# Windowed decode attention and a gated block on one core: one exponential per group with mask products, w4's last rows split over DMA engines, one load for the last rows of wo

## The chip, the core and the metric

The kernel runs on one core of a Trainium2 chip. Its time is device microseconds; the median of three runs of the kernel before is 193.25 us (193.23 to 193.55).

## What is computed

One decode step. A row x of 512 is normalised; s is sliding window attention of 32 heads over the last 4,096 of 32,768 cached positions, with 128 features per head; g is a small gated block of matrix products on the same row; the output is x + s * silu(g). All inputs are bf16.

```python
q = (x @ wq).reshape(...)                     # 32 heads of 128, from xn
k, v = k_cache[:, :, Sk - W:, :], v_cache[:, :, Sk - W:, :]     # W = 4096
scores = einsum("bhqd,bhkd->bhqk", q, k) * Dh ** -0.5
p = softmax(scores, axis=-1)
s = einsum("bhqk,bhkd->bhqd", p, v).reshape(...) @ wo
# the block: h = gelu(layernorm(xn) @ w1), shifted by a position or two;
# with one position nothing of it is left, so hs = 0
x1 = xn + hs
h2 = gelu(layernorm(x1) @ w3) @ w4
out = x + s * silu(x1 + h2)
```

## The kernel before

**Tiling.** The 32 heads go in eight groups of G = 4. A group's K is one tile of 128 partitions by 128 positions by 128 features (4 MB); partition 4b + a holds the positions of head a in block b, so that a partition belongs to one head of the four. V is laid out in the same way. Three K tiles and two V tiles are held at a time.

**Stages of a group.** Step s of the main loop works on the scores of group s, the softmax of group s - 1 and the values of group s - 2 (LAG = 2).

- k_vector (L316 to L323) computes the scores of the first 64 or 80 positions of each partition on VectorE, in four parts: a product with q (L321) and a sum (L323) into S.
- k_turn (L339, L342) and k_scores (L350) compute those of the other 48 or 64: TensorE transposes K, ScalarE copies the result, and TensorE multiplies it with q of all four heads into sT. Each row of sT then has four scores of which one, that of the partition's head, counts. Groups 0 and 7 have 64 positions here and the others 48.
- sm_own (L354 to L359) multiplies sT with the mask par (1 where the head is the partition's) on ScalarE, four instructions. sm_max (L364, L366) adds the four up into S and takes the row's maximum m1.
- sm_turn (L368 to L376) turns m1 onto one partition (TensorE), takes a maximum for each head (mx), and writes minus the scaled maximum into the first row of md, whose four other rows hold 0 on the diagonal and -1e30 off it.
- sm_exp (L378 to L389): a TensorE product of par_t and md gives every partition four offsets, the right one for its own head and about -1e30 for the other heads. ScalarE then makes four exponentials of S, one for each offset, so that those of other heads come out as 0, with their sums.
- sm_den, sm_rden (L394, L399): sums over partitions, reciprocal.
- v_wide (L423 to L433) multiplies pT with V into ov and copies it to SBUF, v_turn (L444) transposes it, v_add (L450) adds up, v_out (L464 to L475) multiplies with the reciprocal into o. For groups 3 to 7 v_out is one instruction on VectorE, for 0 to 2 four on ScalarE.
- ox_spread, ox_pick and y_wide (L478 to L520) bring o into the layout of the product with wo, for heads 0 to 15 (in step 6), 16 to 23 (steps 7 and 8) and 24 to 27 (steps 8 and 9). Heads 28 to 31 go by y_head (L522) with the rows wo_rows. warm (L504) runs matmuls whose result is not used.

**Order.** Order on TensorE, VectorE and ScalarE is that of the program (a manual schedule, L527 to L649), and each engine waits in that order. All large loads but wq are issued by SyncE in the order of the program (L75, L76): w2, w3, w4, then K 0, 1, 2, V 0, K 3, V 1 and so on, each when its buffer is free; wq comes from ScalarE's queue. V 7 is loaded in three pieces, cuts = (0, 64, 96, 128), behind which stand two loads of wo_rows (L542, L543). In step 9 the last piece of V 7 is multiplied by v_part (L458), then v_out(7), four y_head, the product with silu (L651), the sum (L653) and the store.

The order of step 8, and the places where ox_spread follows v_out:

```python
            if h > 0:
                v_add(h - 1)
                v_out(h - 1)
            if s == 6:
                ox_spread(0)
            k_vector(s, kn, 3)
...
        elif s == NG:
            ox_pick(1)
            sm_turn(NG - 1)
            sm_exp(NG - 1)
            y_wide(1, False)
            sm_den(NG - 2)
            sm_rden(NG - 2)
            y_wide(0, False)
            warm(3)
            v_wide(h, v)
```

In step 7, v_add(5), v_out(5), ox_spread(1) and sm_max(7) are the last of VectorE.

Of the kernel before, what the change touches and what calls it, by code (L numbers as in the profile page):

```python
# [8 lines left out]
P = 128  # L9
BF16 = mybir.dt.bfloat16  # L10
FP32 = mybir.dt.float32
ACT = mybir.ActivationFunctionType
# [6 lines left out]
G = 4  # L19
LAG = 2  # L20
K_BUFS = 3
V_BUFS = 2
LATE = 7


@with_exitstack
def kernel(
# [42 lines left out]
    sm_pool = ctx.enter_context(tc.tile_pool(name="sm", bufs=3))  # L70
    small.tile([P, 96], BF16, name="pad")
    wts_guard = tc.tile_pool(name="wts", bufs=1)
    wts = wts_guard.__enter__()

    def load(dst, src):  # L75
        return tc.keep_in_program_order(nc.sync.dma_start(out=dst, in_=src))  # L76
# [14 lines left out]
    load(w4_sb[:, 0:10, :], B_w4[0:10 * P, :].rearrange("(p c) n -> p c n", p=P))  # L91
    load(w4_sb[0:96, 10, :], B_w4[10 * P:F, :])

# [27 lines left out]
    neg_half = const.tile([P, 33], FP32, name="neg_half")  # L121
    nc.vector.memset(neg_half[:], -0.5)

# [104 lines left out]
    shifted_bf = small.tile([P, KC], BF16, name="shifted_bf")  # L228
    nc.vector.memset(shifted_bf[:], 0.0)
    hs_ps = ps_misc.tile([P, KC], FP32, tag="misc", name="hs_ps")  # L230
# [16 lines left out]
    for c in range(KC):  # L247
        wc = w3_sb[:, c, 0:10 * P].rearrange("p (q r) -> p r q", r=10)
        parts = [(j, a_ps[32 * j:32 * j + 1, :, :], wc[:, 3 * j:3 * j + 3, :]) for j in range(3)]
        parts += [(3, a_ps[96:97, 0, :], wc[:, 9, :]), (3, a_ps[96:97, 1, 0:96], w3_sb[:, c, 10 * P:F])]  # L250
        for j, dst, w in parts:
            nc.tensor.matmul(dst, lhsT=z3_bf[:, c:c + 1], rhs=w, start=False, stop=(c == KC - 1),
                             skip_group_check=True)
# [14 lines left out]
    for i, (col, w) in enumerate(terms):  # L268
# [28 lines left out]
                            op=ALU.max)  # L297
    par_t = const.tile([1 + G, PB, G], FP32, name="par_t")
    nc.vector.tensor_scalar(out=par_t[:],
                            in0=ident_f[0:1 + G, 1:1 + G].unsqueeze(1).to_broadcast([1 + G, PB, G]),  # L300
                            scalar1=ident_f[0:1 + G, 0:1], scalar2=None, op0=ALU.add)
    md = const.tile([1 + G, G], FP32, name="md")
    nc.vector.tensor_scalar(out=md[:], in0=ident_f[0:1 + G, 1:1 + G], scalar1=-1.0, scalar2=1e30,
                            op0=ALU.add, op1=ALU.mult)

    st = {}

    def nd(g):
        return 64 if g == 0 or g >= LATE else 80

    def k_open(g):
        st[g] = {
            "sT": ps_s.tile([P, CP - 64, G], FP32, tag="sT", name="sT"),
            "S": sm_pool.tile([P, CP], FP32, tag="S", name="S"),
        }
# [37 lines left out]

    def sm_own(g):  # L354
        s = st[g]
        m = CP - nd(g)
        s["own"] = sm_pool.tile([P, CP - 64, G], FP32, tag="own", bufs=1, name="own")
        for a in range(G):
            nc.scalar.mul(s["own"][:, 0:m, a], s["sT"][:, 0:m, a], par[:, a:a + 1])  # L359

    def sm_max(g):
        s = st[g]
        n = nd(g)
        nc.vector.tensor_reduce(out=s["S"][:, n:CP], in_=s["own"][:, 0:CP - n, :], axis=AX.X, op=ALU.add)  # L364
        s["m1"] = sm_pool.tile([P, 1], FP32, tag="m1", name="m1")
        nc.vector.tensor_reduce(out=s["m1"][:], in_=s["S"][:], axis=AX.X, op=ALU.max)  # L366

    def sm_turn(g):  # L368

        s = st[g]  # L370
        mt_ps = ps_misc.tile([1, P], FP32, tag="misc", name="mt_ps")
        nc.tensor.transpose(mt_ps[:], s["m1"][:], ident_f[:])  # L372
        mx = sm_pool.tile([1, G], FP32, tag="mx", name="mx")
        nc.vector.tensor_reduce(out=mx[:], in_=mt_ps[:].rearrange("r (b a) -> r a b", a=G), axis=AX.X,  # L374
                                op=ALU.max)
        nc.vector.tensor_scalar(out=md[0:1, :], in0=mx[:], scalar1=-scale, scalar2=None, op0=ALU.mult)  # L376

    def sm_exp(g):  # L378
        s = st[g]
        mb_ps = ps_misc.tile([P, G], FP32, tag="misc", name="mb_ps")  # L380
        nc.tensor.matmul(mb_ps[:], lhsT=par_t[:].rearrange("k b a -> k (b a)"), rhs=md[:], start=True,  # L381
                         stop=True)
        mb = sm_pool.tile([P, G], FP32, tag="mb", name="mb")
        nc.scalar.copy(out=mb[:], in_=mb_ps[:])  # L384
        s["pT"] = sm_pool.tile([P, CP, G], BF16, tag="pT", name="pT")
        s["sum"] = sm_pool.tile([P, G], FP32, tag="sum", name="sum")
        for a in range(G):
            nc.scalar.activation(out=s["pT"][:, :, a], in_=s["S"][:], func=ACT.Exp, scale=scale,  # L388
                                 bias=mb[:, a:a + 1], accum_out=s["sum"][:, a:a + 1])  # L389

    def sm_den(g):
        s = st[g]
        s["den"] = ps_misc.tile([P, G], FP32, tag="misc", name="den_ps")
        nc.tensor.matmul(s["den"][:], lhsT=ones_f[:], rhs=s["sum"][:], start=True, stop=True)  # L394

    def sm_rden(g):
        s = st[g]
        s["rden"] = sm_pool.tile([P, G], FP32, tag="rden", name="rden")
        nc.vector.reciprocal(out=s["rden"][:], in_=s["den"][:])  # L399
# [14 lines left out]
    def load_rows(h, n):  # L414
        load(wo_rows[:, h - h_part:h - h_part + n, :],
             A_wo[h * P:(h + n) * P, :].rearrange("(h p) n -> p h n", p=P))
# [29 lines left out]
    def v_add(g):  # L446
        s = st[g]
        if g < NG - 1:
            s["oT"] = sm_pool.tile([P, G], FP32, tag="oT", name="oT")
        nc.vector.tensor_reduce(out=s["oT"][:], in_=s["ot"][:].rearrange("p (x m) -> p m x", m=32)[:, 0:G, :],  # L450
                                axis=AX.X, op=ALU.add)
# [12 lines left out]
    def v_out(g):  # L464
        h = G * g
        b = [i for i, (h0, _) in enumerate(blocks) if h >= h0][-1]
        if b not in o_blk:
            o_blk[b] = sm_pool.tile([P, blocks[b][1]], BF16, tag=f"o{b}", bufs=1, name="o")
        c = h - blocks[b][0]
        if g >= NG - 5:  # L470
            nc.vector.tensor_tensor(out=o_blk[b][:, c:c + G], in0=st[g]["oT"][:], in1=st[g]["rden"][:],
                                    op=ALU.mult)
            return
        for k in range(G):
            nc.scalar.mul(o_blk[b][:, c + k:c + k + 1], st[g]["oT"][:, k:k + 1], st[g]["rden"][:, k:k + 1])  # L475

# [54 lines left out]
    for s in range(NG + LAG):  # L531
# [8 lines left out]
        if last:  # L540
            v = load_kv(v_pool, A_v_cache, h, cuts)
            for r in (H - G, H - 2):  # L542
                load_rows(r, 2)  # L543
        elif h >= 0:
            v = load_kv(v_pool, A_v_cache, h)
# [8 lines left out]
        if s < NG:  # L554
# [32 lines left out]
            k_scores(s, nb - 1)  # L587
            sm_own(s)
            if s == 7:
# [95 lines left out]
```

## Time and profile before

| what | value |
|---|---|
| median of three runs | 193.25 us |
| span of the profiled execution (the page gives this time of it) | 191.2 us |
| TensorE matmul, weight load busy | 116.4, 74.2 us (61, 39%) |
| VectorE busy | 150.9 us (79%) |
| ScalarE busy | 89.2 us (47%) |
| GpSimd busy | 2.3 us (1%) |
| moved by DMA | 79.02 MB, mean 413 GB/s |
| chain that ended last | VectorE 46%, DMA 43%, TensorE 5%, ScalarE 3% |

The page divides the span into 40 slices and gives the busy share of each engine in tenths. The chain of work that ended last is followed back from the last instruction, at each step to what released it. A group of instructions has its line, engine, operation, output and inputs, shape and count, then busy time, mean duration in ns, and the idle time of the engine ahead of it with its cause. A row in order of time has start and length in us. TensorE matmuls are pipelined and their ends are modelled.

### The profile page before, as it was taken

The page shows a single profiled execution, that of the slowest core. Times are in us where ns is not written, and L with a number is a line of the kernel's source. Part 1 is how long each engine was busy: PE and PEld are TensorE (multiplying, and loading weights), DVE is VectorE, ACT ScalarE, POOL GpSimd, SP SyncE. Part 2 cuts the span into 40 slices and gives each one's busy share as a digit, 9 for nine tenths or more (in the row PEclk, how much of TensorE's full clock was granted, in tenths as well). Part 3 has the DMA queues.
Part 4 walks back from the last instruction along what each step waited for, and adds up shares of the span by engine and source line. Part 5 has one row for each costly group of instructions (what it writes and reads, how often), then busy time and mean ns, then how long its engine had stood idle before and what let it go on. Part 6 is the DMA issues. An engine that isn't in the chain of part 4 may idle for free.

```text
span 191.2 us, 2839 instructions
## 1 busy us (share of the span) xinstructions
PE 116.4 (61%) x1159; PEld 74.2 (39%) x1159; DVE 150.9 (79%) x175; ACT 89.2 (47%) x191; POOL 2.3 (1%) x11
## 2 busy tenths in 40 slices
PE   1653754989825368256845772680888189739762
PEld 0430222767614334143334441540763077313322
DVE  1660159979999999999999999999999999980111
ACT  2001370888794076427464564542475148733120
POOL 2110000000000000000000000000000000000000
PEclk9999695555755557955695588557567858975998
DMA  6999999999999999999999999999999998999990
GB/s 211 447 430 404 431 418 439 439 439 437 432 434 439 432 429 432 432 439 432 422 432 432 418 422 418 452 439 435 439 432 434 435 432 372 471 425 405 420 371 32
DMA packets 4572, 79.02 MB, mean 413 GB/s; under 512 B 624, under 2 KB 1232, under 8 KB 1488
## 3 DMA queue, kind: packets, MB, share of 16 engines
q1 hardware_dynamic: 4264, 74.65, 91.6%
q10 hardware_dynamic: 296, 4.20, 5.1%
q8 instruction: 9, 0.15, 0.3%
q14 instruction: 3, 0.02, 0.0%
HBM read 78.84 MB, written 0.00 MB: 412 GB/s over the span
## 4 chain that ended last, share of the span: by engine, by line
DVE 46%; DMA 43%; PE 5%; ACT 3%; issue 1%; SPq 1%; ACTq 0%; DVEq 0%
DMA kv<-in_A_k_cache_dram 31%; DVE S L323 28%; DVE prod L321 15%; DMA kv<-in_A_v_cache_dram 10%; ACT kt L342 3%; DMA x_bf<-in_A_x_dram 2%; PE pt L339 2%; PE ov L427 1%; DVE m L366 1%; DVE S L364 1%; SPq L76 1%; PE sT L350 1%; DVE mx L374 1%; PE oT L461 1%; PE ot_ps L444 0%
## 5 line engine op out<-in xcount | busy, mean ns | idle before, releaser
L323 DVE TENSOR_REDUCE S<-prod 128x20 f32<-128x2560 bf16 (+1 forms) x32 | 86.0, 2686 | 1.1
L342 ACT COPY kt<-pt 128x1024 bf16<-128x1024 bf16 x52 | 51.2, 1013 | 40.4 <-PE pt L339 38.7
L339 PE MATMUL pt<-ident_f,kv 128*128 128x128 f32 x208 | 46.7, 376 | 10.8 <-DMA kv<-in_A_k_cache_dram 10.8
L321 DVE TENSOR_TENSOR prod<-kv,q_bc 128x2560 bf16<-128x2560 bf16 (+1 forms) x32 | 45.4, 1418 | 3.9 <-DMA kv<-in_A_k_cache_dram 3.7
L339 PEld LDWEIGHTS pt<-ident_f,kv 128*128 128x128 f32 x208 | 34.2, 196 | 14.4 <-DMA kv<-in_A_k_cache_dram 10.5
L350 PE MATMUL sT<-q_pair,kt 128*128 128x8 bf16 x416 | 19.4, 170 | 15.7 <-ACT kt L342 15.5
L350 PEld LDWEIGHTS <-kt 128*128 128x128 bf16 x416 | 16.4, 104 | 26.8 <-ACT kt L342 25.8
L427 PE MATMUL ov<-kv,pT 128*16 128x512 bf16 x248 | 22.0, 515 | 1.4 <-DMA kv<-in_A_v_cache_dram 1.4
L388 ACT ACTIVATE pT<-S,mb 128x128 bf16<-128x128 f32 x32 | 13.9, 573 | 0.3
L372 PE MATMUL mt_ps<-ident_f,m 128*1 128x128 f32 x8 | 2.9, 359 | 17.4 <-DVE rden L399 16.9
L433 ACT COPY ov_sb<-ov 128x512 f32<-128x512 f32 x8 | 4.7, 586 | 17.1 <-PE ov L427 17.1
L427 PEld LDWEIGHTS <-pT 128*16 128x16 bf16 x248 | 6.9, 109 | 13.2 <-issue 11.4
L359 ACT ACTIVATE own<-sT,par 128x48 f32<-128x48 f32 (+1 forms) x32 | 7.5, 356 | 3.7 <-PE sT L350 3.7
L444 PE MATMUL ot_ps<-ident_f,ov_sb 128*128 128x128 f32 x32 | 7.1, 359 | 2.9 <-ACT mb L384 1.9
L211 DVE CAST q_row<-qr_ps 128x512 bf16<-128x512 f32 x1 | 0.7, 692 | 9.9 <-PE qr_ps L208 9.9
L388 ACT ACTIVATION_READ_ACCUMULATOR pT<-S,mb 128x1 f32 x32 | 8.3, 258 | 0.0
L372 PEld LDWEIGHTS mt_ps<-ident_f,m 128*1 128x1 f32 x8 | 0.6, 80 | 17.9 <-DVE rden L399 17.2
L399 DVE RECIPROCAL rden<-den_ps 128x4 f32<-128x4 f32 x8 | 1.4, 175 | 7.0 <-PE den_ps L394 7.0
L381 PE MATMUL mb_ps<-md,par_t 5*128 5x4 f32 x16 | 3.9, 311 | 4.1 <-DVE md L376 4.1
L255 ACT ACTIVATE a_row<-a_ps 128x384 bf16<-128x384 f32 x1 | 0.5, 491 | 12.0 <-remote 12.0
L444 PEld LDWEIGHTS ot_ps<-ident_f,ov_sb 128*128 128x128 f32 x32 | 4.5, 178 | 3.9 <-ACT mb L384 2.3
L208 PE MATMUL qr_ps<-wq_sb,xq_bf 128*1 128x512 bf16 x32 | 3.1, 566 | 3.7 <-DMA wq_sb<-in_A_wq_dram 3.7
(122 smaller groups left out, 81.6 us busy)
## 6 DMA issues: line engine op xcount, KB each, us to landing
kv<-in_A_k_cache_dram SPq DMA_DIRECT2D x7, 4096.0 KB, 31.3
kv<-in_A_v_cache_dram SPq DMA_DIRECT2D x7, 4096.0 KB, 30.6
wq_sb<-in_A_wq_dram ACTq DMA_DIRECT2D x1, 4096.0 KB, 17.6
kv<-in_A_k_cache_dram SPq DMA_DIRECT2D x2, 2048.0 KB, 27.4
wo<-in_A_wo_dram SPq DMA_DIRECT2D x1, 2048.0 KB
kv<-in_A_v_cache_dram SPq DMA_DIRECT2D x1, 2048.0 KB
kv<-in_A_v_cache_dram SPq DMA_DIRECT2D x2, 1024.0 KB, 17.6
w_sb<-in_B_w_dram SPq DMA_DIRECT2D x1, 1376.0 KB, 9.1
```

The costliest lines, as they stand in the source:

```text
L321: nc.vector.tensor_tensor(out=prod[:, 0:m, :], in0=kn[:, rows, :], in1=q_bc[:, g:g + 1, :].to_broadcast([P, m, Dh]), op=ALU.mult)
L323: nc.vector.tensor_reduce(out=st[g]["S"][:, rows], in_=prod[:, 0:m, :], axis=AX.X, op=ALU.add)
L339: nc.tensor.transpose(pt[:, i, :], kn[:, c:c + 2, :].rearrange("p c d -> p (c d)").bitcast(FP32), ident_f[:])
L342: nc.scalar.copy(out=kts[b][:, 0:n, :], in_=pt[:, 0:n, :].bitcast(BF16))
L350: nc.tensor.matmul(st[g]["sT"][:, c:c + 2, :].rearrange("p c a -> p (c a)"), lhsT=kt[:, i, l::2], rhs=q_pair[:, g, l, :], start=(l == 0), ...
L359: nc.scalar.mul(s["own"][:, 0:m, a], s["sT"][:, 0:m, a], par[:, a:a + 1])
L372: nc.tensor.transpose(mt_ps[:], s["m1"][:], ident_f[:])
L381: nc.tensor.matmul(mb_ps[:], lhsT=par_t[:].rearrange("k b a -> k (b a)"), rhs=md[:], start=True, stop=True)
L388: nc.scalar.activation(out=s["pT"][:, :, a], in_=s["S"][:], func=ACT.Exp, scale=scale, bias=mb[:, a:a + 1], accum_out=s["sum"][:, a:a + 1])
L427: nc.tensor.matmul(ov[r:r + 4 * G], lhsT=s["pT"][:, c:c + 4, :].rearrange("p i a -> p (i a)"), rhs=v[:, c:c + 4, :], start=(i < 4), stop=( ...
L433: nc.scalar.copy(out=s["ov_sb"][:], in_=ov[:])
L444: nc.tensor.transpose(ot_ps[:, step * j:step * j + P], s["ov_sb"][:, j, :], ident_f[:])
```

## The change

1. sm_own is gone. Its product with par is one VectorE instruction in sm_max, which reads sT in PSUM.
2. The offset of a row is only that of its own head: sm_turn writes a row of 128 values (32 times the four), TensorE spreads it over the partitions, and one exponential per group makes e and one column of sums. Four ScalarE products of e with par make pT. The denominator's matmul takes the sums, spread over 128 columns, and par. par_t and md are gone.
3. v_out of groups 0 to 5 is one GpSimd instruction; groups 6 and 7 stay on VectorE.
4. The 96 rows of w4's last chunk come as two loads, one of 80 rows whose source has the outermost size 5 and one of 16 rows. The rows' order changes with it, and w3's last columns are read in that order too.
5. The four rows of wo_rows come as one load.
6. Buffers: S, rden and oT have eight, own, e and mxr one; the tile pad grows from 192 to 416 bytes per partition. Two memsets move from VectorE to GpSimd.

```diff
-    small.tile([P, 96], BF16, name="pad")
+    small.tile([P, 208], BF16, name="pad")
...
-    load(w4_sb[0:96, 10, :], B_w4[10 * P:F, :])
+    w4_tail = B_w4[10 * P:F, :].rearrange("(i e) n -> e i n", e=TAIL)
+    few = (TAIL - 1) * 16
+    load(w4_sb[0:few, 10, :], w4_tail[0:TAIL - 1])
+    load(w4_sb[few:96, 10, :], w4_tail[TAIL - 1])
...
-    nc.vector.memset(neg_half[:], -0.5)
+    nc.gpsimd.memset(neg_half[:], -0.5)
...
-    nc.vector.memset(shifted_bf[:], 0.0)
+    nc.gpsimd.memset(shifted_bf[:], 0.0)
...
-            "S": sm_pool.tile([P, CP], FP32, tag="S", name="S"),
+            "S": sm_pool.tile([P, CP], FP32, tag="S", bufs=NG, name="S"),
...
-    def sm_own(g):
-        s = st[g]
-        m = CP - nd(g)
-        s["own"] = sm_pool.tile([P, CP - 64, G], FP32, tag="own", bufs=1, name="own")
-        for a in range(G):
-            nc.scalar.mul(s["own"][:, 0:m, a], s["sT"][:, 0:m, a], par[:, a:a + 1])
-
     def sm_max(g):
         s = st[g]
         n = nd(g)
-        nc.vector.tensor_reduce(out=s["S"][:, n:CP], in_=s["own"][:, 0:CP - n, :], axis=AX.X, op=ALU.add)
+        own = sm_pool.tile([P, CP - 64, G], FP32, tag="own", bufs=1, name="own")[:, 0:CP - n, :]
+        nc.vector.tensor_tensor(out=own, in0=s["sT"][:, 0:CP - n, :],
+                                in1=par[:].unsqueeze(1).to_broadcast([P, CP - n, G]), op=ALU.mult)
+        nc.vector.tensor_reduce(out=s["S"][:, n:CP], in_=own, axis=AX.X, op=ALU.add)
...
-        nc.vector.tensor_scalar(out=md[0:1, :], in0=mx[:], scalar1=-scale, scalar2=None, op0=ALU.mult)
+        s["mx"] = sm_pool.tile([1, PB, G], FP32, tag="mxr", bufs=1, name="mxr")
+        nc.vector.tensor_scalar(out=s["mx"][:], in0=mx[:].unsqueeze(1).to_broadcast([1, PB, G]), scalar1=-scale,
+                                scalar2=None, op0=ALU.mult)
 
     def sm_exp(g):
         s = st[g]
-        mb_ps = ps_misc.tile([P, G], FP32, tag="misc", name="mb_ps")
-        nc.tensor.matmul(mb_ps[:], lhsT=par_t[:].rearrange("k b a -> k (b a)"), rhs=md[:], start=True,
-                         stop=True)
-        mb = sm_pool.tile([P, G], FP32, tag="mb", name="mb")
+        mb_ps = ps_misc.tile([P, 1], FP32, tag="misc", name="mb_ps")
+        nc.tensor.matmul(mb_ps[:], lhsT=s["mx"][:].rearrange("k b a -> k (b a)"), rhs=one_f,
+                         start=True, stop=True)
+        mb = sm_pool.tile([P, 1], FP32, tag="mb", name="mb")
         nc.scalar.copy(out=mb[:], in_=mb_ps[:])
+        e = sm_pool.tile([P, CP], BF16, tag="e", bufs=1, name="e")
         s["pT"] = sm_pool.tile([P, CP, G], BF16, tag="pT", name="pT")
-        s["sum"] = sm_pool.tile([P, G], FP32, tag="sum", name="sum")
+        s["sum"] = sm_pool.tile([P, 1], FP32, tag="sum", name="sum")
+        nc.scalar.activation(out=e[:], in_=s["S"][:], func=ACT.Exp, scale=scale, bias=mb[:], accum_out=s["sum"][:])
         for a in range(G):
-            nc.scalar.activation(out=s["pT"][:, :, a], in_=s["S"][:], func=ACT.Exp, scale=scale,
-                                 bias=mb[:, a:a + 1], accum_out=s["sum"][:, a:a + 1])
+            nc.scalar.mul(s["pT"][:, :, a], e[:], par[:, a:a + 1])
...
-        nc.tensor.matmul(s["den"][:], lhsT=ones_f[:], rhs=s["sum"][:], start=True, stop=True)
+        nc.tensor.matmul(s["den"][:], lhsT=s["sum"][:].to_broadcast([P, P]), rhs=par[:],
+                         start=True, stop=True)
...
-        if g >= NG - 5:
+        if g >= NG - 2:
             nc.vector.tensor_tensor(out=o_blk[b][:, c:c + G], in0=st[g]["oT"][:], in1=st[g]["rden"][:],
                                     op=ALU.mult)
             return
-        for k in range(G):
-            nc.scalar.mul(o_blk[b][:, c + k:c + k + 1], st[g]["oT"][:, k:k + 1], st[g]["rden"][:, k:k + 1])
+        nc.gpsimd.tensor_tensor(out=o_blk[b][:, c:c + G], in0=st[g]["oT"][:], in1=st[g]["rden"][:], op=ALU.mult)
...
-            for r in (H - G, H - 2):
-                load_rows(r, 2)
+            load_rows(H - G, G)
...
-            sm_own(s)
```

More of the change, by code (lines that the diff above doesn't have):

```diff
@@ L23 @@
 LATE = 7
+TAIL = 6
 @with_exitstack
@@ L249 @@
         parts = [(j, a_ps[32 * j:32 * j + 1, :, :], wc[:, 3 * j:3 * j + 3, :]) for j in range(3)]
-        parts += [(3, a_ps[96:97, 0, :], wc[:, 9, :]), (3, a_ps[96:97, 1, 0:96], w3_sb[:, c, 10 * P:F])]
+        parts += [(3, a_ps[96:97, 0, :], wc[:, 9, :]), (3, a_ps[96:97, 1, 0:96].rearrange("o (e i) -> o e i", e=TAIL),
+                   w3_sb[:, c, 10 * P:F].rearrange("p (i e) -> p e i", e=TAIL))]
         for j, dst, w in parts:
@@ L297 @@
                             op=ALU.max)
[L298 to L304, printed above, removed]
     st = {}
@@ L393, in sm_den @@
         s["den"] = ps_misc.tile([P, G], FP32, tag="misc", name="den_ps")
-        nc.tensor.matmul(s["den"][:], lhsT=ones_f[:], rhs=s["sum"][:], start=True, stop=True)
+        nc.tensor.matmul(s["den"][:], lhsT=s["sum"][:].to_broadcast([P, P]), rhs=par[:],
+                         start=True, stop=True)
     def sm_rden(g):
         s = st[g]
-        s["rden"] = sm_pool.tile([P, G], FP32, tag="rden", name="rden")
+        s["rden"] = sm_pool.tile([P, G], FP32, tag="rden", bufs=NG, name="rden")
         nc.vector.reciprocal(out=s["rden"][:], in_=s["den"][:])
@@ L448, in v_add @@
         if g < NG - 1:
-            s["oT"] = sm_pool.tile([P, G], FP32, tag="oT", name="oT")
+            s["oT"] = sm_pool.tile([P, G], FP32, tag="oT", bufs=NG, name="oT")
         nc.vector.tensor_reduce(out=s["oT"][:], in_=s["ot"][:].rearrange("p (x m) -> p m x", m=32)[:, 0:G, :],
```

## The prediction

> **What bounds the kernel now.** I read the page first: the slices of the span, then the chain of work that ended last, then the waits, and last the order in time of VectorE and TensorE where the stages meet. In the slices, each column is 4.8 us:
>
> ```profile
> DVE  1660159979999999999999999999999999980111
> DMA  6999999999999999999999999999999998999990
> GB/s 211 447 430 404 431 418 439 439 439 437 432 434 439 432 429 432 432 439 432 422 432 432 418 422 418 452 439 435 439 432 434 435 432 372 471 425 405 420 371 32
> ```
>
> Two rows are full. The DMA engines are busy from 5 to 186 us and move 79.02 MB at about 435 GB/s; no kernel that loads these bytes ends much sooner. But VectorE is full too, from the start of group 1 (42 us) to the end of group 7 (171 us). The question is who has slack against whom. VectorE's rows where groups 5 and 6, 6 and 7 meet, and after group 7 (start, length, engine, line, operation):
>
> ```profile
> 132.96 0.34 DVE L364 TENSOR_REDUCE S<-own 128x48 f32<-128x192 f32 x1
> 133.34 0.29 DVE L366 TENSOR_REDUCE m<-S 128x1 f32<-128x128 f32 x1
> 134.17 1.49 DVE L321 TENSOR_TENSOR prod<-kv,q_bc 128x2560 bf16<-128x2560 bf16 x1 [0.55 <-DMA kv<-in_A_k_cache_dram]
> ...
> 153.87 0.29 DVE L366 TENSOR_REDUCE m<-S 128x1 f32<-128x128 f32 x1
> 154.07 1.22 DVE L321 TENSOR_TENSOR prod<-kv,q_bc 128x2048 bf16<-128x2048 bf16 x1
> ...
> 170.29 0.29 DVE L366 TENSOR_REDUCE m<-S 128x1 f32<-128x128 f32 x1
> ```
>
> A group takes VectorE 18.2 us (60.7 to 78.9, 78.9 to 97.2 and so on) and its K and V take the DMA 19.4 us. Yet VectorE starts late and only catches up at group 6: 0.55 us of idle before it, none before group 7. Its whole reserve is 0.55 us. What follows the last maximum is in TensorE's rows:
>
> ```profile
> 171.79 0.55 PE L381 MATMUL mb_ps<-md,par_t 5*128 5x4 f32 x2 [0.65 <-DVE md L376]
> ...
> 175.56 1.07 PE L507 MATMUL wm<-zero_bf 128*128 128x512 bf16 x3
> 176.56 1.90 PE L427 MATMUL ov<-kv,pT 128*16 128x512 bf16 x32
> ...
> 181.50 1.04 PE L427 MATMUL ov<-kv,pT 128*16 128x512 bf16 x16 [1.02 <-DMA kv<-in_A_v_cache_dram]
> ...
> 183.93 0.61 PE L427 MATMUL ov<-kv,pT 128*16 128x512 bf16 x8 [0.41 <-DMA kv<-in_A_v_cache_dram]
> ...
> 186.38 0.96 PE L461 MATMUL oT<-pT,kv 128*128 128x4 bf16 x32 [0.17 <-DMA kv<-in_A_v_cache_dram]
> ```
>
> From mb_ps on TensorE runs nearly without a gap through y_wide(1), y_wide(0) and warm into v_wide(6), which starts at 176.56, just as group 6's V is in. The DMA is what ends last only by these three waits: 1.02 + 0.41 + 0.17 = 1.60 us. So a maximum of group 7 that comes up to 1.6 us later is free, and beyond that each 1 us costs 1 us.
>
> **The change part by part.** The sum is made against the profiled execution (span 191.2 us) and added to the median of the runs, 193.25 us; the 2.05 us between are around the span and stay.
>
> *The product sT x par moves from ScalarE (32 x 356 ns of L359) to VectorE, ahead of the L364 sum.* No row shows it, but these do (count, busy, mean ns):
>
> ```profile
> L492 DVE TENSOR_TENSOR pick<-ox_ps,mh 128x256 f32<-128x256 f32 x1 | 0.4, 414 | 0.0
> L492 DVE TENSOR_TENSOR pick<-ox_ps,mh 128x64 f32<-128x64 f32 x1 | 0.2, 215 | 0.0
> L299 DVE TENSOR_SCALAR par_t<-ident_f 5x128 f32<-5x128 f32 x1 | 0.3, 266 | 0.0
> L376 DVE TENSOR_SCALAR md<-mx 1x4 f32<-1x4 f32 x8 | 1.2, 156 | 0.3
> L178 POOL TENSOR_TENSOR ln_rstd_x<-ln_rstd_x,neg_half 128x1 f32<-128x1 f32 x1 | 0.6, 554 | 5.7 <-DVE ln_rstd_x L176 5.7
> ```
>
> pick is the same form: a float32 product of PSUM with a broadcast mask. Its line through 215 and 414 ns gives 348 ns at 192 elements and 414 at 256. The Trainium skill (VectorE: DVE Perf Modes, the section on the TRN2 errata) prices an instruction with a PSUM source at 120 cycles plus one per element at 0.96 GHz: 325 and 392 ns. The same page places VectorE nearer SBUF and ScalarE nearer PSUM, which speaks against this move; pick is the evidence that decides, and the rule would make my eight products only 0.18 us cheaper. The sum waits for its product, and dependent rows start 0.03 to 0.04 us after the one before (132.96, 133.34), so 0.38 us for groups 1 to 6 and 0.44 for groups 0 and 7: 3.16 us in all. Bounds: 2.76 (the rule, a little less) and 3.44 (gaps of 0.07). Nothing hides it, since VectorE is full.
>
> *The offset row (L376) becomes 128 wide instead of 4.* Between 156 + 40 ns and the 266 of par_t, which also reads a pointer scalar; I take +0.07, eight times: 0.56 us (bounds 0.32 and 0.88).
>
> *v_out of groups 0 to 5 goes to GpSimd.* Groups 0 to 2 were on ScalarE (12 x 289 ns), off the path; 3 to 5 were on VectorE. Groups 3 and 5 are followed at once by ox_spread on VectorE, which now waits for GpSimd; behind it in VectorE's queue stand k_vector(6, 3) and sm_max(7). Before, add to spread took 147.44 to 147.95, 0.51 us. Now: add 0.21, hop 0.08 (7.42 to 7.50, the row of L178), product, hop 0.04. The nearest row for the product is L178 itself, 554 ns, a power; a plain product of four columns may cost as little as the 0.20 of a memset. So +0.02 to +0.37 each[...]. I take 0.30, nearer to the row. Twice: 0.60. Group 4's goes without a waiter and saves about 0.08.
>
> The chain, then: products of groups 0 to 5, 0.44 + 5 x 0.38 = 2.34, and five offset rows, 0.35, make 2.69 us; less the 0.55 of idle, group 6 starts 2.14 late. Group 6 adds 0.07 + 0.30 + 0.38 = 0.75, group 7 0.07 + 0.30 + 0.44 - 0.08 = 0.73, the last offset row 0.07. mb_ps comes **3.69 us later**, v_wide(6) with it. Less 1.60 us of waits: **+2.1 us**. By the bounds, 2.49 to 4.43 us late, hence +0.9 to +2.8.
>
> *One exponential.* ScalarE loses 24 of 32 exponentials (573 + 258 ns each) and gets 32 products of 128 elements at some 0.45 us (379 ns at 64). It ends up about 9 us less busy, and earns nothing: it waits 38.7 us for TensorE's transposes as it is, and no wait for exp stands on the tail. The mb and den matmuls stay two passes each.
>
> *w4's tail.* A 1 KB packet took 46 ns in the trace's packet records. Five engines get 17 rows for 6, +0.51 us; eleven get 1 for 6, -0.23 us. All engines then run without a gap to the end, so these shifts stay until the last V lands. The engines' last marks are 2.0 us apart (184.31 to 186.33), because each 16 KB instruction fetch holds one engine back about 1.5 us. Which are the five? The skill (DMA: Bandwidth & Descriptors, on how many engines a DMA uses) says the lowest-numbered, and x_row's four rows would be on four of them. Followed packet by packet, two of those four are early at the end and two were held by fetches, 0.24 us short of the last. So +0.27 (0.24 short, 0.51 more); bounds -0.23 and +0.51. The same skill's rule to use all 16 engines speaks against the split; here it decides nothing, because TensorE comes later than these packets: zero on the sum, and the figure counts if VectorE's delay is hidden. w4 is used at 25.4 us and lands at 21.2, so its own landing has cover.
>
> *wo_rows as one load.* The first product on it now waits for all four rows: they land 1.28 us after V's last piece, the product came 1.26 after: +0.06, hidden likewise. The w4 load that is added and the one dropped shift the reuse of DMA semaphores by one: the first K load would wait for x_bf (landed 4.7 us) behind a queue that is full until 20 us. Nothing. The two memsets on GpSimd, the deeper buffers (no wait on S, rden or oT is in the list of waits) and the pad: nothing.
>
> *The loads.* K buffers come free up to 3 us later and the last V is issued about 3 us after 166.55. What stands in the queue then lasts until 174.6, so the DMA doesn't run dry.
>
> **The rivals.** (1) Not slower: the delay stays under 1.6 us because the products cost VectorE almost nothing, and the DMA still ends last. Deciding point: 3.69 - 1.60 over eight products, some 0.26 us less each, that is 0.1 us for a product. Time then 193.25 + 0.33 = 193.6 with the held engines among the five, 193.25 - 0.17 = 193.1 without. Against it: pick's 414 ns. For it: ScalarE's relief could close gaps that I don't see. (2) The split doesn't go to the engines it names, or fetches fall otherwise: under (1) only, 193.1 to 193.8. (3) The DMA runs dry: needs 8 us of delay at 166.55; then 198 and more. Against it: I find 3.
>
> **How the numbers follow.** Forecast 0.78: 195.3. Rival (1) 0.13, half of it near 193.1 and half near 193.6 (with (2) inside it); (3) 0.03; the rest, 0.06, a tail that TensorE's clock stretches past 196.5. Bounds +0.9 to +2.8 are 194.1 to 196.1; the granted clock in the tail slices lies between 0.5 and 0.9, so I add 0.4 each side: 193.7 to 196.5. A measurement can tell about 0.2%, 0.4 us: faster than that 0.06, within it 0.10, slower 0.84.
>
> **What would show it.** VectorE's last maximum near 174 us instead of 170.3, no idle before group 6, a product row of 350 ns, TensorE without the three waits for V, and the chain of waits ending in VectorE and TensorE rows instead of V's landing. If V's last landing still ends the chain, or the maximum comes before 172.2, the forecast is wrong.

## The result, and the profile after

The changed kernel takes 196.31 us (median of 6 runs, 195.34 to 197.35); the kernel before, run beside it, 193.43 us (6 runs, 193.23 to 193.94). The ratio is 1.0151, 95% interval 1.0133 to 1.0168: slower by 2.9 us, where 195.3 (193.7 to 196.5) was forecast. The profiled execution took 196.46 us, with a span of 194.6 us against 191.2.

First the slices of the changed kernel, 4.9 us each, the same rows as before:

```profile
DVE  0560169989999999999999999999999998971021
DMA  6998999999999999999999999999999999999930
GB/s 205 482 427 381 418 428 458 431 431 436 431 431 438 438 421 440 431 431 438 428 431 431 431 428 401 461 431 428 431 431 431 428 431 402 461 418 399 418 122 4
```

VectorE (DVE) is full for longer, and the DMA, which was busy to the last slice but one, is now at 3 there: the loads end and the kernel runs on. Next the groups that the change adds or alters (count, busy time, mean ns):

```profile
L356 DVE TENSOR_TENSOR own<-sT,par 128x192 f32<-128x192 f32 x6 | 2.1, 349 | 0.0
L371 DVE TENSOR_SCALAR mxr<-mx 1x128 f32<-1x128 f32 x8 | 1.7, 214 | 0.3
L356 DVE TENSOR_TENSOR own<-sT,par 128x256 f32<-128x256 f32 x2 | 0.8, 416 | 0.0
L472 POOL TENSOR_TENSOR o<-oT,rden 128x4 bf16<-128x4 f32 x6 | 5.6, 940 | 154.4 <-DVE oT L448 154.4
```

The products take what pick's rows said (348 and 414 forecast, 349 and 416 measured). VectorE in order of time, at the same places as before:

```profile
135.37 0.35 DVE L356 TENSOR_TENSOR own<-sT,par 128x192 f32<-128x192 f32 x1
...
136.34 1.48 DVE L319 TENSOR_TENSOR prod<-kv,q_bc 128x2560 bf16<-128x2560 bf16 x1
...
156.74 1.21 DVE L319 TENSOR_TENSOR prod<-kv,q_bc 128x2048 bf16<-128x2048 bf16 x1
...
172.88 0.22 DVE L448 TENSOR_REDUCE oT<-ot_ps 128x4 f32<-128x64 f32 x1 [0.91 <-PE ot_ps L442]
...
174.46 0.29 DVE L360 TENSOR_REDUCE m<-S 128x1 f32<-128x128 f32 x1
```

The wait for K ahead of group 6 (0.55 us) is gone and the group starts 2.17 us later; group 7 starts 2.67 later, the last maximum 4.17 later. Between these two stands something new: VectorE waits 0.91 us for TensorE. TensorE's own rows say why, and show the tail:

```profile
160.46 0.38 PE L391 MATMUL den_ps<-par,sum 128*128 128x4 f32 x2 [1.56 <-DVE oT L448]
...
164.00 0.37 PE L366 MATMUL mt_ps<-ident_f,m 128*1 128x128 f32 x1 [1.13 <-DVE rden L397]
...
167.83 3.59 PE L425 MATMUL ov<-kv,pT 128*16 128x512 bf16 x32
...
175.92 0.55 PE L377 MATMUL mb_ps<-ones_f,mxr 1*128 1x1 f32 x2 [0.71 <-DVE mxr L371]
...
179.68 1.46 PE L504 MATMUL wm<-zero_bf 128*128 128x512 bf16 x3
181.07 2.54 PE L425 MATMUL ov<-kv,pT 128*16 128x512 bf16 x32
...
185.57 1.04 PE L425 MATMUL ov<-kv,pT 128*16 128x512 bf16 x16
...
187.42 0.60 PE L425 MATMUL ov<-kv,pT 128*16 128x512 bf16 x8
...
189.82 0.94 PE L459 MATMUL oT<-pT,kv 128*128 128x4 bf16 x32
```

The three waits for V are gone from the last three rows: TensorE now comes after the loads. And the same 32 matmuls of v_wide, 1.90 us for group 5 and for group 6 before, take 3.59 and 2.54 us. TensorE's rows of before, where it neither waits ahead of sm_den(5) nor runs slow in v_wide(5):

```profile
159.28 0.36 PE L394 MATMUL den_ps<-sum,ones_f 128*128 128x4 f32 x2
...
164.60 1.90 PE L427 MATMUL ov<-kv,pT 128*16 128x512 bf16 x32
```

The granted clock explains it: in the profile's clock records it changes between full and half, at moments that lie multiples of 3.41 us apart in every run. Before, it was full from 159.0 to 169.3 us and again from 176.1; after, it is half from 161.9 to 172.2 and from 175.6 to 182.4. Two of these windows of the changed kernel, with the time that TensorE was busy in them, its matmuls, the granted clock, and the DMA's share and GB/s:

```profile
158.50:161.90 3.40, 1.84 (x27) 1.00 0.97 417
161.90:165.30 3.40, 1.79 (x23) 0.50 1.02 430
```

In the first TensorE waits 1.56 us for VectorE, whose add of group 4 is late (the row of L391 above; the add starts at 160.19 us, at 157.53 before); busy for only 1.84 us, it has half the clock in the next. The window of before at that place had 3.06 us of work, and the clock stayed full:

```profile
159.03:162.40 3.37, 3.06 (x47) 1.00 0.82 352
```

### The profile page after: what moved, and what is told of

The parts are those of the page before. It is cut to its first block, busy times and chain, and to the rows that moved or that the text cites. A ratio compares the mean times of both kernels' runs of the same rounds, so it can differ in the third digit from the quotient of the medians.

```text
span 194.6 us, 2790 instructions
## 1 busy us (share of the span) xinstructions
PE 121.8 (63%) x1159; PEld 77.0 (40%) x1159; DVE 153.9 (79%) x176; ACT 81.8 (42%) x131; POOL 8.2 (4%) x19
## 4 chain that ended last, share of the span: by engine, by line
DVE 62%; DMA 21%; issue 7%; PE 7%; POOL 1%; ACT 1%; ACTq 0%; POOLq 0%; DVEq 0%
DVE S L321 36%; DVE prod L319 18%; DMA kv<-in_A_k_cache_dram 18%; DMA x_row<-in_A_x_dram 3%; PE ov L425 2%; PE yr_ps L515 2%; DVE S L358 2%; DVE own L356 1%; PE wm L504 1%; DVE m L360 1%; DVE mxr L371 1%; DVE mx L368 1%; PE ot_ps L442 1%; POOL o L472 1%; PE oT L459 0%
## 5 line engine op out<-in xcount | busy, mean ns | idle before, releaser
L337 PE MATMUL pt<-ident_f,kv 128*128 128x128 f32 x208 | 47.6, 382 | 5.7 <-DMA kv<-in_A_k_cache_dram 5.7
L337 PEld LDWEIGHTS pt<-ident_f,kv 128*128 128x128 f32 x208 | 34.8, 198 | 8.9 <-DMA kv<-in_A_k_cache_dram 5.1
L425 PE MATMUL ov<-kv,pT 128*16 128x512 bf16 x248 | 24.6, 564 | 0.0
L472 POOL TENSOR_TENSOR o<-oT,rden 128x4 bf16<-128x4 f32 x6 | 5.6, 940 | 154.4 <-DVE oT L448 154.4
L386 ACT ACTIVATE pT<-e,par 128x128 bf16<-128x128 bf16 x32 | 11.7, 556 | 0.3
L377 PE MATMUL mb_ps<-ones_f,mxr 1*128 1x1 f32 x16 | 4.2, 332 | 5.6 <-DVE mxr L371 5.6
L380 ACT COPY mb<-mb_ps 128x1 f32<-128x1 f32 x8 | 1.3, 159 | 13.2 <-PE mb_ps L377 13.2
L377 PEld LDWEIGHTS mb_ps<-ones_f,mxr 1*128 1x128 f32 x16 | 3.8, 290 | 7.0 <-PE sT L348 5.3
```

Of the source, the lines that this page charges most:

```text
L337: nc.tensor.transpose(pt[:, i, :], kn[:, c:c + 2, :].rearrange("p c d -> p (c d)").bitcast(FP32), ident_f[:])
L377: nc.tensor.matmul(mb_ps[:], lhsT=s["mx"][:].rearrange("k b a -> k (b a)"), rhs=one_f, start=True, stop=True)
L386: nc.scalar.mul(s["pT"][:, :, a], e[:], par[:, a:a + 1])
L425: nc.tensor.matmul(ov[r:r + 4 * G], lhsT=s["pT"][:, c:c + 4, :].rearrange("p i a -> p (i a)"), rhs=v[:, c:c + 4, :], start=(i < 4), stop=( ...
L472: nc.gpsimd.tensor_tensor(out=o_blk[b][:, c:c + G], in0=st[g]["oT"][:], in1=st[g]["rden"][:], op=ALU.mult)
```

## The experiments

Each was timed against the kernel before on the same chip (medians of 193.40 to 193.57 us).

**1. The changed kernel with the product back on ScalarE** (e1): sm_own as before and called where it was; all else of the change stays.

```diff
-        nc.vector.tensor_tensor(out=own, in0=s["sT"][:, 0:CP - n, :],
-                                in1=par[:].unsqueeze(1).to_broadcast([P, CP - n, G]), op=ALU.mult)
...
+        for a in range(G):
+            nc.scalar.mul(s["own"][:, 0:m, a], s["sT"][:, 0:m, a], par[:, a:a + 1])
```

> The changed kernel with one part undone: the product of sT with par is on ScalarE again, ahead of the sum on VectorE; all else of the change stays. Theory (VectorE's added product makes the last maximum late, and TensorE's tail with it): of the 4.17 us by which the last maximum came later, the eight products are 3.16; what is left is eaten by the 0.55 us of idle and the 1.60 us of waits for V, the DMA ends last again, at 193.43 less the 0.16 us by which V landed earlier: 193.3 us. Rival A (the hop through GpSimd, the wider offset row or the single exponential cost it): 195 us or more. Rival B (TensorE's clock in the tail is what costs it, whatever VectorE does): 194.5 us or more.

Measured: 193.24 us (193.15 to 193.72), ratio 0.9988 (0.9979 to 0.9997). All of the loss is gone. The last maximum is back at 170.49 us, and the waits for V are back in TensorE's rows:

```profile
181.74 1.04 PE L429 MATMUL ov<-kv,pT 128*16 128x512 bf16 x16 [0.89 <-DMA kv<-in_A_v_cache_dram]
...
184.16 0.61 PE L429 MATMUL ov<-kv,pT 128*16 128x512 bf16 x8 [0.41 <-DMA kv<-in_A_v_cache_dram]
...
186.61 0.96 PE L463 MATMUL oT<-pT,kv 128*128 128x4 bf16 x32 [0.16 <-DMA kv<-in_A_v_cache_dram]
```

**2. The kernel before with only the product on VectorE** (e2).

```diff
-            sm_own(s)
...
+        nc.vector.tensor_tensor(out=own, in0=s["sT"][:, 0:CP - n, :],
+                                in1=par[:].unsqueeze(1).to_broadcast([P, CP - n, G]), op=ALU.mult)
         nc.vector.tensor_reduce(out=s["S"][:, n:CP], in_=own, axis=AX.X, op=ALU.add)
```

> The kernel before with one part of the change: the product of sT with par is on VectorE; nothing else is changed. Theory: the last maximum 3.16 - 0.55 = 2.6 us late, less 1.60 us of waits is +1.0, and up to 1.1 more where TensorE's clock is low in the tail as it was in the changed kernel: 194.4 to 195.6 us. Rival A (GpSimd, offset row or exponential): 193.4 us, no change.

Measured: 196.67 us (196.22 to 197.35), ratio 1.0154 (1.0137 to 1.0170), above my range. The product alone makes the whole loss; with experiment 1 this is shown from both sides. My range had TensorE's low clock in the tail alone. Here it is half from 162.4 to 182.9 us, and so ahead of the last maximum too: v_wide(5) takes 3.59 us, v_wide(6) 2.50, and VectorE waits 1.44 us for TensorE, so that the last maximum comes at 174.95 us, 4.66 late. (The profiled execution is the slowest of the five.)

```profile
167.94 3.59 PE L423 MATMUL ov<-kv,pT 128*16 128x512 bf16 x32
...
173.44 0.23 DVE L446 TENSOR_REDUCE oT<-ot_ps 128x4 f32<-128x64 f32 x1 [1.44 <-PE ot_ps L440]
...
181.60 2.50 PE L423 MATMUL ov<-kv,pT 128*16 128x512 bf16 x32
```

**3. The kernel before with only the new loads** (e3): w4's rows in two loads, wo_rows in one.

```diff
-    load(w4_sb[0:96, 10, :], B_w4[10 * P:F, :])
+    load(w4_sb[0:few, 10, :], w4_tail[0:TAIL - 1])
+    load(w4_sb[few:96, 10, :], w4_tail[TAIL - 1])
...
-                load_rows(r, 2)
+            load_rows(H - G, G)
```

> The kernel before with the loads of the change alone: w4's last rows as 80 on five engines and 16 on all, wo_rows as one load. The DMA ends last here. Theory after the result (V's last piece landed 0.16 us earlier in the changed kernel): -0.16 and +0.06 for the four rows that must be there together: 193.3 us. The reading of the prediction (two held engines among the five): +0.27 + 0.06: 193.8 us.

Measured: 193.58 us (193.38 to 194.21), ratio 1.0009 (1.0000 to 1.0018), between the two expectations, which were 0.5 us apart. V's last piece lands at 186.23 us, against 186.33 in the profile of before; y_ps then waits 0.34 us for wo_rows, where before it waited 0.26 for o, and starts at the same time (187.58 for 187.59). By the medians the loads cost 0.1 us, if anything, and which of the two does can't be told here.

**4. The changed kernel without warm(3) ahead of v_wide(6)** (e4).

```diff
             y_wide(0, False)
-            warm(3)
             v_wide(h, v)
```

> The changed kernel without the three matmuls of warm (whose result is not used) ahead of v_wide(6). Theory (TensorE's chain from the last maximum on sets the end): they stood on it for 1.46 us, so 196.3 - 1.4 = 194.9 us, if what follows runs at the same clock. Rival (they hold the clock up, and without them what follows takes longer): 196 us or more. If the DMA set the end: no change.

Measured: 196.05 us (195.59 to 196.98), ratio 1.0134 (1.0112 to 1.0156): only 0.26 us less, where 1.4 was expected, and the intervals of the two ratios overlap. The 1.46 us of warm are saved, but v_wide(6) takes 2.97 us instead of 2.54:

```profile
179.76 2.97 PE L425 MATMUL ov<-kv,pT 128*16 128x512 bf16 x32
```

So the unused matmuls were partly paid back by the clock, and my reading that they are plain cost was wrong. The profiled execution, the fastest of the five, is 0.87 us faster than the changed kernel's; why the medians differ by less is not shown.

**5. The changed kernel with unused matmuls in step 7's gaps** (e5): three of 512 columns ahead of sm_den(5), two ahead of sm_turn(6), where TensorE waited 1.56 and 1.13 us.

```diff
+                for _ in range(3):
+                    nc.tensor.matmul(wm7[:], lhsT=zero_bf[:], rhs=zero_bf[:].unsqueeze(1).to_broadcast([P, 4, P]),
+                                     start=True, stop=True)
                 sm_den(h)
...
                 keys(4, nb - 2)
+                for _ in range(2):
+                    nc.tensor.matmul(wm7[:], lhsT=zero_bf[:], rhs=zero_bf[:].unsqueeze(1).to_broadcast([P, 4, P]),
+                                     start=True, stop=True)
                 sm_turn(s - 1)
```

> The changed kernel with five matmuls more in step 7, three ahead of sm_den(5) and two ahead of sm_turn(6), where TensorE stands idle for 1.56 and 1.13 us; their result is not used. Theory (VectorE's lateness makes TensorE wait in step 7, its granted clock falls to a half, v_wide(5) takes 3.59 us for 1.90 and puts VectorE's add of group 5 off by 0.91): the clock stays up, v_wide(5) takes about 1.9 us, the last maximum comes some 0.9 us earlier, and 195.3 to 195.8 us result. Rival (the clock is none of the cause; VectorE's rows alone set it): 196.3 us or a little more.

Measured: 194.71 us (194.20 to 195.43), ratio 1.0060 (1.0039 to 1.0081): 1.6 us less than the changed kernel, by adding work, and below the range I expected. The clock is full from 160.0 to 166.9 us, v_wide(5) starts 0.9 us earlier (though it still takes 3.54, where I expected 1.9), and:

```profile
171.92 0.23 DVE L448 TENSOR_REDUCE oT<-ot_ps 128x4 f32<-128x64 f32 x1 [0.19 <-PE ot_ps L442]
...
173.50 0.29 DVE L360 TENSOR_REDUCE m<-S 128x1 f32<-128x128 f32 x1
```

```profile
166.93 3.54 PE L425 MATMUL ov<-kv,pT 128*16 128x512 bf16 x32
...
180.22 2.03 PE L425 MATMUL ov<-kv,pT 128*16 128x512 bf16 x32
```

VectorE's wait falls from 0.91 to 0.19 us, the last maximum comes 0.96 earlier, and v_wide(6) takes 2.03. V's last landing doesn't move (186.19 us for 186.17), so the loads have no part in it. About 1.6 of the 2.9 us were thus the clock's, in this arrangement. The 1.2 us that stay roughly fit VectorE's own work: the last maximum is still 3.21 us late, 1.6 more than the loads cover.

**6. The changed kernel with 76 chunks on VectorE in groups 1 to 6, not 80** (e6).

```diff
-        return 64 if g == 0 or g >= LATE else 80
+        return 64 if g == 0 or g >= LATE else 76
```

> The changed kernel with 76 instead of 80 of a partition's 128 positions on VectorE in groups 1 to 6 (nd), the other 52 by TensorE and ScalarE. Theory (VectorE is the bound, ScalarE has time to spare): four positions are 4 x 4.27 / 20 = 0.85 us a group on VectorE, 5 us in all, more than the 4.2 by which it was late; VectorE waits for K again, the DMA ends last: 193.3 us. Rival (TensorE and ScalarE become the bound with a seventh batch): 195 us or more.

Measured: 194.72 us (194.52 to 195.08), ratio 1.0064 (1.0048 to 1.0080). That is neither theory's number. Its trace shows VectorE no longer late: the last maximum is at 170.81, v_wide(6) starts at 176.90 and takes 1.90. What is late is a transfer. TensorE's rows, and the DMA queues between 182 and 185 us:

```profile
185.23 0.61 PE L425 MATMUL ov<-kv,pT 128*16 128x512 bf16 x8 [1.87 <-DMA kv<-in_A_v_cache_dram]
186.53 1.12 PE L442 MATMUL ot_ps<-ident_f,ov_sb 128*128 128x128 f32 x4 [0.69 <-ACT ov_sb L431]
```

```profile
q1 hardware_dynamic: 246, 1.21, 98.2%
q8 instruction: 1, 0.02, 2.1%
```

The second row of the first fence runs at half clock (1.12 us for the 0.65 of experiment 1), granted from 186.5 us on, after that wait. The second fence has one packet of queue 8: a fetch of instructions (16 KB, 0.99 us), which starts at 183.12 us. In experiment 1 the last two fetches of this size start at 176.01 and 187.00, and none between. After this one, fifteen of the sixteen landing marks of V's second piece (the trace has sixteen for such a load, read here as one for each DMA engine) lie within 1.83 us, as in the first piece, and the sixteenth at 3.29: one DMA engine is 1.5 us later than any other. v_wide's second piece starts 1.07 us later than in experiment 1, and with the half clock behind it the last product starts 1.51 later. The changed size gives TensorE 36 more matmuls, so the fetch comes earlier in time. That was a guess at this point; experiments 9, 11 and 12 test it.

**7. The kernel before with the product on VectorE in groups 0 to 2 only** (e7).

```diff
+        if g < 3:
+            nc.vector.tensor_tensor(out=own, in0=s["sT"][:, 0:CP - n, :],
+                                    in1=par[:].unsqueeze(1).to_broadcast([P, CP - n, G]), op=ALU.mult)
...
-            sm_own(s)
+            if s >= 3:
+                sm_own(s)
```

> The kernel before with the product on VectorE in groups 0 to 2 only, on ScalarE in the others. Theory (a reserve of 0.55 us of idle and 1.60 us of waits): 0.44 + 2 x 0.38 = 1.20 us late, less 0.55, is 0.65 us at group 6, inside the waits: 193.5 us, no change. Rival (no reserve: any lateness of VectorE costs TensorE's clock in step 7): 194.2 us or more.

Measured: 193.59 us (193.01 to 194.03), ratio 1.0000 (0.9987 to 1.0013). The reserve is there:

```profile
134.95 1.48 DVE L321 TENSOR_TENSOR prod<-kv,q_bc 128x2560 bf16<-128x2560 bf16 x1
...
171.67 0.23 DVE L456 TENSOR_REDUCE oT<-ot_ps 128x4 f32<-128x64 f32 x1 [1.44 <-PE ot_ps L450]
...
172.71 0.29 DVE L372 TENSOR_REDUCE m<-S 128x1 f32<-128x128 f32 x1
```

Group 6 starts 0.78 us later: three products (1.2 us by the forecast's costs) less the 0.55 of idle make 0.65. But in this execution the clock is half from 151.3 to 178.6 us, VectorE waits 1.44 us for TensorE, and the last maximum is 2.42 us late. That is more than the loads cover, and it shows: the waits for V are gone, and the last piece of V is multiplied from 187.03 us on, 0.65 later than before:

```profile
187.03 0.95 PE L467 MATMUL oT<-pT,kv 128*128 128x4 bf16 x32
```

The execution took 193.94 us. Seven of the fourteen runs lie at 193.77 us and more and seven at 193.40 and less, so the median falls between two groups. It says that three products cost nothing that can be told; it doesn't say that a half clock costs nothing.

**8. The changed kernel with v_out on VectorE in all groups** (e8).

```diff
-        if g >= NG - 2:
+        if True:
```

> The changed kernel with v_out of all groups on VectorE, none on GpSimd. The prediction took 0.30 us for each of the two places where VectorE waits for GpSimd: 195.7 us if that was so. After the result (0.53 us from add to spread, with 0.51 before): 196.3 us, or a little more, since groups 0 to 2 and 4 now cost VectorE 0.1 us each.

Measured: 196.65 us (196.29 to 196.84), ratio 1.0158 (1.0140 to 1.0177), not faster than the changed kernel. The hop through GpSimd cost nothing that shows: from the add to the spread it is 0.45 us here and 0.53 in the changed kernel, and the four v_out instructions that GpSimd takes without a waiter give that back (group 6 starts at 136.85 us here, 0.51 later than in the changed kernel).

**9, 11, 12. Experiment 1's kernel with matmuls that compute some scores twice** (e9, e11, e12): six, two or twelve more in each of groups 1 to 6 (the diff is that of six; the other two have 1 and 6 in place of the 3).

```diff
+        more = [(0, 0), (0, 1)] * 3 if b == 0 and 0 < g < LATE else []
-        for i in range((c1 - c0) // 2):
-            for l in range(2):
+        for i, l in more + [(i, l) for i in range((c1 - c0) // 2) for l in range(2)]:
```

> The changed kernel with the product back on ScalarE, and in each of groups 1 to 6 six matmuls of eight columns more, on the first pair of score columns, which are then computed again: 36 in all, the number that the run with 76 chunks adds. VectorE's work is left as it was. Theory (the shortfall of the run with 76 is an instruction fetch: TensorE's ninth 16 KB fetch comes at about its 1128th matmul, at 187.0 us without and at 183.1 with 36 more, and there it holds one DMA engine, so that a piece of the last V lands 1.3 us late): 194.3 to 194.9 us, the fetch near 183 us, a wait of TensorE for V of about 1.9 us at the second or the third piece. Rival (the shortfall comes from VectorE's work or from TensorE's longer groups in themselves): 193.2 to 193.5, since 36 short matmuls are some 2 us of TensorE spread over six groups, in which it waits for other engines.

Measured: 194.77 us (194.09 to 195.25), ratio 1.0062 (1.0043 to 1.0081). The fetch starts at 183.22 us, and TensorE's wait is that of experiment 6:

```profile
185.33 0.61 PE L430 MATMUL ov<-kv,pT 128*16 128x512 bf16 x8 [1.91 <-DMA kv<-in_A_v_cache_dram]
```

The last maximum is at 171.21, within the cover. So the shortfall of experiment 6 needs none of VectorE's work.

> The changed kernel with the product back on ScalarE and two matmuls more in each of groups 1 to 6, 12 instead of the 36 of the last run but one; some scores are computed twice. Theory (what cost 1.3 us was that TensorE's ninth fetch of instructions fell ahead of the last V's packets): with 12 more it comes at the matmul that stands 12 ahead of the one at 187.0 us, that is at about 186.5 us, when the last V is in: 193.2 to 193.6 us. Rival (the added matmuls cost in proportion, 1.3 us x 12/36): 193.6 to 193.8, with the waits for V unchanged.

Measured: 193.24 us (193.04 to 193.60), ratio 0.9989 (0.9981 to 0.9998). The fetch starts at 186.96, not at 186.5 as I had counted, and so after V; TensorE's waits for V are 0.59, 0.41 and 0.16 us.

> The same with twelve matmuls more in each of groups 1 to 6, 72 in all. The ninth fetch then comes 72 matmuls ahead of the one at 187.0 us, near 178 to 180 us, ahead of all three pieces of the last V. Theory (the fetch holds one DMA engine for good, wherever it falls while the queue runs without a gap): 194.2 to 195.0 us, the long wait for V at the first piece already. Rival 1 (only a fetch in the middle of the last pieces costs): 193.2 to 193.6. Rival 2 (the cost is the matmuls' own, in proportion): 195.8 and more.

Measured: 194.75 us (194.61 to 195.45), ratio 1.0080 (1.0061 to 1.0098). The fetch starts at 180.31; each of V's three pieces now has one landing mark of sixteen at 3.44 to 3.46 us and the others within 1.95. The long wait at the first piece that I expected isn't there (0.31 us), since TensorE itself comes 1.55 us later than in experiment 1; but V's last landing, 187.72 us, still ends last:

```profile
187.76 0.96 PE L464 MATMUL oT<-pT,kv 128*128 128x4 bf16 x32 [0.17 <-DMA kv<-in_A_v_cache_dram]
```

Twice the matmuls of experiment 9 cost the same: it isn't the matmuls, but whether this ninth fetch falls ahead of the last V. Not every fetch there costs: the changed kernel's eighth starts at 179.18 us and experiment 8's at 180.15, and no landing mark of V stands apart in either. In experiment 8 seven marks of V's first piece come early, by 180.13 us, and six of the second, so that fetch seems to have held an engine that was ahead, and the ninth one that was already behind. The trace doesn't name the engines.

**10. Experiment 1's kernel with the old loads** (e10): what stays of the change is one exponential, v_out on GpSimd, the memsets and the buffers.

```diff
-    load(w4_sb[0:few, 10, :], w4_tail[0:TAIL - 1])
-    load(w4_sb[few:96, 10, :], w4_tail[TAIL - 1])
+    load(w4_sb[0:96, 10, :], B_w4[10 * P:F, :])
...
-            load_rows(H - G, G)
+                load_rows(r, 2)
```

> The changed kernel with the product back on ScalarE and with the two changes to loads taken back (w4's 96 rows as one load over all engines, the rows of wo as two loads): what is left of the change is one exponential with products by masks, v_out on GpSimd, the memsets and the buffers. Theory (the loads cost nothing or 0.1%, as the run with them alone showed; the small gain over the kernel before comes from the softmax and v_out): 193.0 to 193.3 us. Rival (the gain of 0.12% came from the split of w4): 193.4 to 193.6, as the kernel before.

Measured: 193.12 us (192.89 to 193.81), ratio 0.9985 (0.9973 to 0.9997). So the loads were not what made experiment 1 a little faster; that leaves the rest of the change, and which part of it wasn't tried. Experiments 1 and 10 lie below both kernels. The gain over the kernel before, 0.2 to 0.4 us, is about as large as can be told.

## Why the prediction was right, and where its sizes were off

The direction and the mechanism hold: the product on VectorE makes the last maximum late, the reserve is 0.55 us ahead of group 6 and 1.60 us in the waits for V, and what goes beyond it ends the kernel (experiments 1, 2 and 7). The time is 1.0 us above the forecast and inside its range, by 0.2 us; two of the six runs lie above it. That it stayed inside is partly luck: the hop was taken 0.5 us too dear, and a term of 0.91 us and the slower tail were missing. By its steps:

- *Products*: 349 and 416 ns, as forecast. With the offset rows (214 ns against 156, +0.06 for +0.07) group 6 starts 2.17 us late, for 2.14.
- *Hop through GpSimd*: 0.60 us in the sum, nothing that shows (experiment 8). Its product took 0.20 us where VectorE waits for it, less than the row of L178 that I leaned on (554 ns). From the add to the spread it was 0.02 and 0.08 us more than before, near the lower of the two bounds.
- *From group 7's start to the last maximum*: 0.73 us was in the sum, 1.50 came. The step assumed that nothing but VectorE's own rows stands there. VectorE's wait for ot_ps, 0.91 us, is missing in it: v_wide(5) ran at half clock. This and the hop together bring mb_ps 4.13 us late, for 3.69.
- *The tail from mb_ps on* was taken to keep its length. warm and v_wide(6) grew by 0.39 and 0.64 us, at half clock. So v_part starts 3.44 us late (189.82 for 186.38): 4.13 + 0.39 + 0.64 - 1.60, less 0.12 in gaps that closed. The forecast had 2.1.
- *The clock*, which the sum left at its old state, is thus the term that was missing. The forecast had it only as 0.4 us at each side and as a case of 6 in 100. Filling TensorE's gaps in step 7 takes 1.6 us back (experiment 5). The time is also less certain: the runs of the changed kernel spread over 2.0 us and those of before over 0.7. TensorE now lies on the path and the moments of its clock's changes differ between the traces, which would explain it; no experiment shows it.
- *w4's split* was costed at zero behind VectorE's delay, and at +0.27 on V's landing. After, V's last piece lands 0.16 us earlier (186.17), and in experiment 1, 0.23 later (186.56); with the old loads it is 186.33 in one profile (before) and 186.02 in another (experiment 10), so this is no more than it moves anyway. Whether the five engines are early or late at the end is not settled. The price is at most 0.2% (experiment 3's interval).
- *wo_rows* as one load: hidden after; a wait of 0.31 to 0.34 us on it shows where V ends last (experiments 1 and 3).
- *One exponential*: ScalarE is 7.4 us less busy (81.8 for 89.2), for about 9, but not where the forecast had it. It counted mean durations, and these overlap: before, an exponential started every 0.39 us (107.12, 107.53, 107.91) though it and its sum take 573 and 258 ns; the products start every 0.3 us and take 556. So the 32 exponentials kept ScalarE busy for 15.2 us, and the eight with the 32 products for 16.9 (a table load of 1.3 us in both). The relief is sm_own's 7.5 us and v_out's 2.6. It earns little; at most it has a part in the 0.4 us of experiment 10.
- *The DMA doesn't run dry*: right. V's last landing hardly moves though V is issued 4.9 us later (172.71 for 167.79).

What stays open: the clock of a window follows the work in the one ahead of it, but not always. In the traces of before and after, from 150 us on, it rose from half after windows with about 3.2 us of work and more, and fell from full after 1.9 us and less; but in experiment 7 two windows with 3.42 and 3.31 us, from 158.1 to 165.0, left it at half. Over all the traces, from 35 us on, every full window with less than 1.95 us of work was followed by half, those with 1.95 to 2.54 us by either, and no amount of work was sure to bring full clock back. So a forecast can say that a stage is exposed, not which windows it will lose.

## What to carry to other kernels

Before work is moved to an engine that is full, count its reserve at each place where it could still catch up, here 0.55 us of idle and 1.60 us of waits for the last load; up to that the move is free, and beyond it every us counts. A delay that opens gaps on TensorE can cost as much again through its clock (1.6 of the 2.9 us here), so a forecast should say what the later stages take at half clock. And a change of 36 matmuls somewhere early can cost 1.5 us at the end (experiment 9 for 1) by moving a fetch of instructions in front of the last load: when a size change has an odd result, look where the fetches fall.

## What the runs showed of the hardware

**A fetch of instructions can leave one DMA engine late to the end.** It moves 16 KB, in 0.93 to 1.15 us while the loads run. In experiment 12, where the queues run without a gap behind it, the same lateness of 1.5 us is in all three pieces of V. Where the ninth fetch falls ahead of the last V, V's last piece lands 0.9 to 1.4 us later (187.47 to 187.72 us in experiments 6, 9 and 12, against 186.32 and 186.56 in 11 and 1).

**GpSimd's small product waits for VectorE's large one.** Two of the changed kernel's six, each with the row of VectorE beside it:

```profile
93.92 1.38 POOL L472 TENSOR_TENSOR o<-oT,rden 128x4 bf16<-128x4 f32 x1 [80.62 <-DVE oT L448]
...
149.95 0.20 POOL L472 TENSOR_TENSOR o<-oT,rden 128x4 bf16<-128x4 f32 x1 [17.30 <-DVE oT L448]
```

```profile
93.76 1.48 DVE L319 TENSOR_TENSOR prod<-kv,q_bc 128x2560 bf16<-128x2560 bf16 x1
...
150.19 0.42 DVE L479 TENSOR_TENSOR spread<-o,mt 128x256 bf16<-128x256 bf16 x1 [0.31 <-POOL o L472]
```

The first starts while VectorE multiplies two operands from SBUF and ends at 95.30 us, 0.06 after VectorE's row; the second, with VectorE waiting, takes 0.20 us. Four of the six are of the first kind (1.11 to 1.38 us). The Trainium skill (GPSIMD Engine Reference, Specifications) says that GpSimd shares SBUF interfaces with VectorE and contends with its instructions that have two SBUF inputs; here each of the four ends 0.05 to 0.06 us behind VectorE's row, so that it is a wait until the instruction ends. Nobody waited for these four.

**The clock of TensorE moves in windows of 3.41 us.** All its changes in these runs lie on such a grid, between 0.5 and 1.0 (in each trace; where the grid lies differs between traces). The Trainium skill (TensorE: Matmul & The Clock Gate, Part 1) has the same window and the two states; it gives half clock after an idle window and full clock after a busy one. Here a window with 1.84 us of work was followed by half, so waits of about half a window were enough, and experiment 7's half clock through 27.3 us, with two nearly full windows in it, doesn't fit the second part.
